# RWKV-7 attention into a mixture of experts: early loads, order of two small products, and the last store, all changed

## The chip, the cores and the metric

The program runs on one core of a Trainium2 chip. The time is that of the device for one execution, in microseconds (us). Ten executions of the kernel before took 1162.47 to 1171.4 us, with a median of 1168.91.

Five engines run their own instruction streams and wait for each other through semaphores: TensorE (PE; its weight loads are listed apart as PEld), VectorE (DVE), ScalarE (ACT), GpSimd (POOL) and SyncE (SP), which here only issues DMAs. Matrix products go to PSUM, everything else lies in SBUF.

## The reference

Two blocks follow each other. The first is a recurrence over 768 tokens for 4 batches and 8 heads of 40 numbers; the second is a mixture of 4 experts over the resulting 3072 rows of 320 numbers.

```python
for t in range(S):                                   # r,k,v,w,a,b: (4, 8, 768, 40)
    y[:, :, t] = einsum('bhd,bhde->bhe', rt, state)
    Sa = einsum('bhde,bhe->bhd', state, at)
    state_decay = state * wt[:, :, None, :] - einsum('bhd,bhe->bhde', Sa, bt)
    state = state_decay + einsum('bhd,bhe->bhde', vt, kt)

x = y.transpose(0, 2, 1, 3).reshape(3072, 320)       # w1: (4, 320, 1024), w2: (4, 1024, 320)
p = domain_probs / (domain_probs.sum(-1, keepdims=True) + 1e-9)
for e in range(4):
    h = maximum(x @ w1[e], 0)
    out += p[:, e:e + 1] * (h @ w2[e])
```

All of it is float32.

## The kernel before, in words

**Units.** The 768 tokens are cut into 12 chunks of 64. A unit is one chunk of two batches, so that 2 x 64 tokens fill the 128 partitions; there are 24 units, two to a chunk. The recurrence is solved inside a chunk with matrix products, and the state of each batch is carried from chunk to chunk.

**Stages of a unit.** They are generators, advanced step by step by `run(gen, n)`.
- `within` (L338 on) needs nothing of the state. It loads nothing itself; it turns the inputs W, A, B, K, V, R of its unit (tiles `natW` and so on), forms decayed keys, and the score matrices F, ET and EV (products `pw`, `pg`, `pRT`, `pVT`, `pAT`, `pNT`, `pKT`, `pc`, `pfe`, `pev`).
- `substitute` (L440 on) inverts 32 x 32 triangles, on GpSimd for all units but the first two.
- `merge` (L490 on) joins the inverses to 64 x 64. Its first step transposes them on VectorE (`Qc`, `QTc`). Its second step is the product `pY` (L510), copied by ScalarE to `Yq` in two copies (L516). Its third step is the product `pQ` (L522), which reads `Yq`, copied by ScalarE into `QT` in two copies (L527).
- `step` (L530 on) goes on with the state. Its first step is the product `prn` (the state against the gathered keys, and the state turned), from which VectorE makes `RH`. Its second step is `psat`, which reads `RH` and `QT`; then `pxr`, `pdy`, and the new state and output.

**Experts.** The output of a unit (first two units) or of a chunk (later) goes through the mixture. `up` (L646 on) makes the hidden layer from one piece of the first weights (L238 loads a piece, 512 KB and twice 64 KB). Down weights are loaded once, 1280 KB an expert (L255). For chunks, the product with the down weights is done in seven half-size products instead of eight: `down_1` makes three of them, `down_2` four, each over the sums of `add_weights` and `add_h` (L763); the products are at L769, and VectorE adds them, scaled by the gate, to the output tile `osb` (L680). The expert work is cut into pieces in the list `todo`; `mix(n)`, called by `gap`, puts n of them between the steps of the recurrence.

**What sets the order.** The program text, for the most part: instructions go to each engine in the order in which they are written, with some moved by a scheduler, and those in `keep_in_program_order` fixed. In the loop over u, iteration u advances `within` of unit u + 2 (`w`), `merge` (`m`) and the first two steps of `step` (`s_next`) of unit u + 1, and the rest of `step` of unit u. For u < 5 (`early`) the merge is placed later than for u of 5 and above.

**Loads.** All DMAs before are issued by SyncE, in one queue, in order. Eight semaphores are used in turn, so that a DMA is issued only when the eighth one before it has landed. Weights and attention inputs of the first units share that queue. `load_probs` (L206) loads the probabilities.

**The end.** After the loop, the last chunk's last expert runs `down_2`: products `p75` and `p26`, two additions each, then `store` (L682 on), two DMAs (one a batch) for each of the two output tiles.

Of the kernel before, what the change touches and what calls it, by code (L numbers as in the profile page):

```python
# [15 lines left out]
def kernel(  # L16
# [34 lines left out]
    nc = tc.nc  # L51

    B, H, S, D = r.shape
    E, DM, F = moe_w1.shape
    P = 128
    L = 64
# [11 lines left out]
    def big(name):  # L68
# [6 lines left out]
        out=ident[:], in_=ident[:], pattern=[[1, P]], compare_op=ALU.is_equal, fill=0.0,  # L75
# [5 lines left out]
    for t, n, op in ((upf, L, ALU.is_gt), (diagf, Q, ALU.is_equal)):  # L81
        nc.vector.memset(t[:], 1.0)
        for q in range(P // n):
            o = slice(q * n, (q + 1) * n)
            nc.gpsimd.affine_select(
                out=t[o], in_=t[o], pattern=[[1, n]], compare_op=op, fill=0.0, base=0, channel_multiplier=-1,
# [132 lines left out]
    def load_piece():  # L219

        k = len(pieces)
        e, x = k // 2 % E, k % 2
        if k in in_sums:
            t = sums[in_sums[k]]
        else:
            t = sb.tile([P, PIECE], FP32, name="w1p", tag="w1p", bufs=2)
        q = Piece()
        q.main = t[:, 0:2 * HF * P].rearrange("p (g c) -> p g c", g=2)
        q.last = t[:, 2 * HF * P:PIECE].rearrange("p (f c) -> p f c", c=P)
        cols = slice(x * HF * P, (x + 1) * HF * P)  # L230
        moves = [(q.main, moe_w1[e, 0:2 * P, cols].rearrange("(g p) c -> p g c", p=P))]
        for i in range(2):
            half_cols = slice((2 * x + i) * HF // 2 * P, (2 * x + i + 1) * HF // 2 * P)
            moves.append(
                (q.last[i * DT:(i + 1) * DT], moe_w1[e, 2 * P:DM, half_cols].rearrange("d (f c) -> d f c", c=P))
            )
        for to, src in moves:
            tc.keep_in_program_order(nc.sync.dma_start(out=to, in_=src))  # L238
        pieces.append(q)
# [14 lines left out]
    def load_w2(e):  # L254
        tc.keep_in_program_order(nc.sync.dma_start(out=w2_sb[e][:], in_=moe_w2[e].rearrange("(f p) d -> p f d", p=P)))  # L255
# [416 lines left out]
    def scale(q, e, minus=False):  # L672
        return (minus_gate if minus else gate)[:, q.c, q.bp, e:e + 1]

    def add(to, p, sc, start=False):

        if start:
            nc.vector.tensor_scalar(out=to, in0=p, scalar1=sc, scalar2=None, op0=ALU.mult)
        else:
            nc.vector.scalar_tensor_tensor(out=to, in0=p, scalar=sc, in1=to, op0=ALU.mult, op1=ALU.add)  # L680

    def store(q, osb):  # L682
        for i in range(2):
            row = q.b[i] * S + q.c * L
            nc.sync.dma_start(out=out[row:row + L, :], in_=osb[i * L:(i + 1) * L, :])

    def outputs():
        return sb.tile([P, DM], FP32, name="osb", tag="osb", bufs=2)
# [35 lines left out]
    def of_w2(e, q, x):  # L724
        return w2_sb[e][:, q * HF:(q + 1) * HF, x * HD:(x + 1) * HD]

    def of_sums(e, n):
        return sums[e][:, n * HF * HD:(n + 1) * HF * HD].rearrange("p (f d) -> p f d", d=HD)
# [14 lines left out]
    def mixture_of_chunk(qs, xT):  # L743

        hs, a_sums, osb = {}, {}, []
        at = 2 * E * (qs[0].c + 1)

        def ups(e, x):
            hs[e, x] = up(at + 2 * e + x, xT, 2 * P, P)
            used(at + 2 * e + x + 1)  # L750

        def of_h(e, s, x):
            return hs[e, x][:, :, s * P:(s + 1) * P]

        def add_h(e):
            a = {(s, x): of_h(e, s, x) for s in range(2) for x in range(2)}
            for n, x, y, op in (
                (1, a[0, 0], a[1, 1], ALU.add), (7, a[0, 1], a[1, 1], ALU.subtract),
                (5, a[0, 0], a[0, 1], ALU.add), (2, a[1, 0], a[1, 1], ALU.add),
                (6, a[1, 0], a[0, 0], ALU.subtract),  # L760
            ):
                t = a_sums[e, n] = sb.tile([P, HF, P], FP32, name=f"a{n}")
                nc.vector.tensor_tensor(out=t[:], in0=x, in1=y, op=op)  # L763

        def products(name, *terms):
            p = ps.tile([P, len(terms) * HD], FP32, name=name, tag="mm", bufs=3)
            for n, (a, b) in enumerate(terms):
                for f in range(HF):
                    nc.tensor.matmul(  # L769
                        out=p[:, n * HD:(n + 1) * HD], lhsT=a[:, f, :], rhs=b[:, f, :],  # L770
                        start=(f == 0), stop=(f == HF - 1),
                    )
            return p

        left, right, wide = slice(0, HD), slice(HD, DM), slice(0, DM)

        def down_1(e):
            p = products(
                "p431", (of_h(e, 1, 1), of_w2(e, 1, 0)), (of_h(e, 0, 0), of_w2(e, 0, 1)),
                (a_sums[e, 1], of_sums(e, 0)),  # L780
            )
            if e == 0:
                osb.extend(outputs() for _ in qs)

            for q, o in zip(qs, osb):
                add(o[:], p[:, wide], scale(q, e), e == 0)
            for q, o, cols in zip(qs, osb, (left, right)):
                add(o[:, cols], p[:, DM:DM + HD], scale(q, e))

        def down_2(e):  # L790
            p75 = products("p75", (a_sums[e, 7], of_sums(e, 2)), (a_sums[e, 5], of_w2(e, 1, 1)))
            p26 = products("p26", (a_sums[e, 2], of_w2(e, 0, 0)), (a_sums[e, 6], of_sums(e, 1)))
            for q, o, p, cols, n in ((qs[0], osb[0], p75, left, 1), (qs[1], osb[1], p26, right, 0)):
                add(o[:], p[:], scale(q, e))
                add(o[:, cols], p[:, n * HD:(n + 1) * HD], scale(q, e, minus=True))
            if e == E - 1:
                for q, o in zip(qs, osb):
                    store(q, o)


        before = last[:]
        for e in range(E):
            todo.append(lambda e=e: ups(e, 0))
            if before:
                todo.append(before[0])
                todo.append(lambda e=e: ups(e, 1))
                todo.append(lambda e=e, then=before[1]: (then(), add_h(e)))
            else:
                todo.append(lambda e=e: (ups(e, 1), add_h(e)))
            before = [lambda e=e: down_1(e), lambda e=e: down_2(e)]  # L810
        last[:] = before

    todo, last = [], []
# [1 line left out]
    def mix(n):  # L815

        for piece in todo[:n]:
            piece()
        del todo[:n]

    def run(gen, n=99):
        for _ in range(n):
            if next(gen, gen) is gen:
                break
# [21 lines left out]
    keep_warm(4)  # L846
    run(ws[0], 1)
    load(units[1], "ABKVR")
    for n in range(4):
        load_piece()  # L850
        if n == 1:
            load_w2(0)
    load_probs()
    run(ws[1], 1)
    run(ws[0], 2)
# [3 lines left out]
    m, s = merge(units[0]), begin_step(0)  # L859
    run(m, 1)  # L860
    run(ws[0])
    load(units[2], "WVR")
    load_w2(1)
    run(ws[1], 1)
    keep_warm(36)
    run(ws[1], 2)
# [13 lines left out]
    m, s = merge(units[1]), begin_step(1)  # L880
# [18 lines left out]
    for u in range(1, NU):  # L899
        q = units[u]  # L900
        m = s_next = w = iter(())
        if u + 1 < NU:
            m, s_next = merge(units[u + 1]), begin_step(u + 1)
        if u + 2 < NU:
            w = within(units[u + 2])

        def gap(n, pieces=None):
            at = 4 * u + n
            run(sum_ops, sums_at.get(at, 0))
            mix((1 if at in sparse else 2) if pieces is None else pieces)  # L910

        run(w, 1)
        run(w_next)
        run(s, 1)
        gap(0)


        early = u < 5
        if early:
            run(s, 1)  # L920
        run(w, 1)
        run(s)
        if u == 1:
            mixture_of_unit(q)
        elif q.bp:
            mixture_of_chunk(units[u - 1:u + 1], chunks_x[q.c])
        run(w, 1)
        if not early:
            run(m, 1)
        gap(1)  # L930

        if u + 3 < NU:
            load(begin(u + 3), srcs)
        run(w, 2)
        if not early:
            run(m, 1)
            run(s_next, 1)
            run(m)
        gap(2)

        if early:
            run(m, 1)
        run(w, 1)
        if not early:
            run(s_next, 1)
        if u + 2 < NU:
            substitute(units[u + 2], nc.gpsimd)
        if early:
            run(m, 1)
            run(s_next, 1)  # L950
            run(m)
            gap(3, 1)
            run(s_next, 1)
            mix(0 if 4 * u + 3 in sparse else 1)
        else:
            gap(3)
        s, w_next = s_next, w
# [31 lines left out]
```

## Time and profile before

| | |
|---|---|
| median of ten executions | 1168.91 us |
| profiled execution | 1170.02 us |
| its span, first to last instruction | 1168.3 us |
| mean granted clock of TensorE | 0.987 |
| TensorE busy | 1140.0 us (98%) |
| VectorE, ScalarE, GpSimd busy | 693.7, 385.5, 470.4 us |
| read from HBM | 97.04 MB |

The profile describes one execution. A wait is listed as "engine tile line <- what ended it: us in total, times, longest". A timeline line has start, length, engine, line, instruction, "out <- in", shapes and a count, and in brackets the idle time of the engine just before. Busy time of TensorE counts a product from its start to a modelled end; products overlap, so that the sum of lengths is more than the time. The clock is that which the chip granted to TensorE, where 1.00 is full speed.

### The profile page before, as it was taken

What the parts mean: (1) busy time and instruction counts of PE and PEld (TensorE: products, weight loads), DVE (VectorE), ACT (ScalarE), POOL (GpSimd) and SP (SyncE); (2) the same over time, 40 slices, a digit from 0 to 9 for tenths busy, and PEclk for the clock granted to TensorE, in tenths of its full rate; (3) what the DMA queues carried; (4) which work ended last, traced back from release to release, by engine and by line L of the source; (5) the groups of instructions that cost most, each with busy time, mean ns of one, the idle gap of its engine ahead of it and who ended that gap; (6) DMA issues with size and microseconds to landing.
All of it is one profiled execution on the core that took longest, in us unless ns stands there. A gap on an engine that the chain in (4) does not pass through costs nothing.

```text
span 1168.3 us, 38755 instructions
## 1 busy us (share of the span) xinstructions
PE 1140.0 (98%) x16400; PEld 1018.4 (87%) x16400; DVE 693.7 (59%) x1465; ACT 385.5 (33%) x961; POOL 470.4 (40%) x1218
## 2 busy tenths in 40 slices
PE   7898999999999999999999999999999999999998
PEld 6787887789898998989989998989989898998887
DVE  7565447766566656756655756666566567543333
ACT  2332444333333333342333333333323423321110
POOL 4005645562542733624625526427336255250000
PEclk8899999999999999999999999999999999999999
DMA  4695424323333243333333342332433331221330
GB/s 67 177 284 107 109 60 106 84 65 97 79 91 86 76 114 73 89 93 85 98 95 81 92 103 59 105 84 79 109 76 91 92 101 51 76 87 52 103 91 12
DMA packets 218693, 107.45 MB, mean 92 GB/s; under 512 B 163688, under 2 KB 191896, under 8 KB 218520
## 3 DMA queue, kind: packets, MB, share of 16 engines
q1 hardware_dynamic: 218520, 104.97, 34.8%
q8 instruction: 130, 2.13, 0.8%
q14 instruction: 43, 0.35, 0.1%
HBM read 97.04 MB, written 3.93 MB: 86 GB/s over the span
## 4 chain that ended last, share of the span: by engine, by line
PE 92%; DMA 2%; SPq 2%; ACT 2%; issue 1%; DVE 1%; DVEq 0%; ACTq 0%
PE ph L662 29%; PE p L769 29%; PE ph L654 9%; PE pdy L327 3%; PE po L703 2%; PE pfe L327 2%; PE psat L327 2%; SPq L188 2%; PE prn L327 2%; PE pxr L327 2%; PE pQ L522 1%; PE pc L327 1%; PE pY L510 1%; PE pev L327 1%; DMA w<-in_moe_w_dram 1%
## 5 line engine op out<-in xcount | busy, mean ns | idle before, releaser
L662 PE MATMUL ph<-xT,w1p 128*128 128x256 f32 (+1 forms) x1520 | 343.3, 379 | 0.0
L471 POOL TENSOR_TENSOR Z<-M,Z 128x62 f32<-128x62 f32 (+7 forms) x352 | 168.7, 479 | 405.7 <-DVE M L464 379.8
L662 PEld LDWEIGHTS ph<-xT,w1p 128*128 128x128 f32 x1520 | 274.4, 191 | 62.6 <-issue 25.2
L763 DVE TENSOR_TENSOR a<-hs 128x512 f32<-128x512 f32 x220 | 154.6, 720 | 190.9 <-ACT hs L667 190.9
L484 POOL TENSOR_TENSOR Z<-Z 128x31 f32<-128x31 f32 (+7 forms) x704 | 241.6, 343 | 55.2
L667 ACT ACTIVATE hs<-ph 128x512 f32<-128x512 f32 (+1 forms) x208 | 117.1, 564 | 304.2 <-PE ph L662 303.7
L769 PE MATMUL p<-sums,a 128*128 128x160 f32 x1056 | 164.8, 299 | 0.0
L680 DVE SCALAR_TENSOR_TENSOR osb<-p,gate,osb 128x320 f32<-128x320 f32 (+1 forms) x242 | 108.2, 485 | 92.5 <-PE p L769 88.3
L769 PEld LDWEIGHTS p<-sums,a 128*128 128x128 f32 x1056 | 152.9, 190 | 2.2
L654 PE MATMUL ph<-xT,w1p 64*128 64x256 f32 (+1 forms) x760 | 110.4, 397 | 0.6 <-ACT hs L667 0.6
L769 PE MATMUL p<-w,hs 128*128 128x160 f32 x704 | 102.9, 299 | 0.0
L769 PE MATMUL p<-w,a 128*128 128x160 f32 x704 | 102.8, 299 | 0.0
L769 PEld LDWEIGHTS p<-w,hs 128*128 128x128 f32 x704 | 100.2, 190 | 2.2
L769 PEld LDWEIGHTS p<-w,a 128*128 128x128 f32 x704 | 98.0, 190 | 0.0
L503 POOL COPY QT<-QTc 32x256 f32<-32x256 f32 x96 | 38.8, 404 | 107.1 <-DVE QTc L497 97.3
L654 PEld LDWEIGHTS ph<-xT,w1p 64*128 64x128 f32 x760 | 67.9, 187 | 13.1 <-issue 2.1
L448 DVE STREAM_TRANSPOSE M<-blocks 128x1024 f32<-128x1024 f32 x24 | 47.0, 1957 | 30.7 <-ACT blocks L445 30.0
L365 DVE RECIPROCAL gp<-gp 128x320 f32<-128x320 f32 x24 | 51.4, 2140 | 0.0
L419 ACT COPY F<-pfe 128x256 f32<-128x256 f32 x48 | 15.5, 375 | 90.7 <-PE pfe L327 90.7
L369 ACT COPY RT<-pRT 128x512 f32<-128x512 f32 x24 | 14.1, 586 | 93.4 <-PE pRT L295 93.3
L595 ACT COPY RS<-pxr 64x256 f32<-64x256 f32 x88 | 32.2, 366 | 34.6 <-issue 25.3
L327 PE MATMUL pdy<-VC,k_tok 64*64 64x104 f32 (+1 forms) x768 | 39.5, 263 | 2.5 <-issue 2.5
(143 smaller groups left out, 1428.2 us busy)
## 6 DMA issues: line engine op xcount, KB each, us to landing
w1p<-in_moe_w_dram SPq DMA_DIRECT2D x95, 512.0 KB
w1p<-in_moe_w_dram SPq DMA_DIRECT2D x190, 64.0 KB
w<-in_moe_w_dram SPq DMA_DIRECT2D x4, 1280.0 KB
sums<-in_moe_w_dram SPq DMA_DIRECT2D x9, 512.0 KB
natW<-in_w_dram SPq DMA_DIRECT2D x48, 80.0 KB
natA<-in_a_dram SPq DMA_DIRECT2D x48, 80.0 KB
natB<-in_b_dram SPq DMA_DIRECT2D x48, 80.0 KB
natK<-in_k_dram SPq DMA_DIRECT2D x48, 80.0 KB
```

Source lines behind the costliest of these rows:

```text
L327: nc.tensor.matmul(out=p[row][half(col), lo + at * out_cols:lo + (at + 1) * out_cols], lhsT=lhsT, rhs=rhs, start=(n == 0), stop=(n == len( ...
L365: nc.vector.reciprocal(out=gp[:], in_=gp[:])
L448: ins = nc.vector.transpose(out=M[:], in_=cols)
L471: ins = eng.tensor_tensor(out=Z[:, 1:3, 0:n, j + 1:Q], in0=M[:, j:j + 2, None, j + 1:Q].to_broadcast([P, 2, n, m]), in1=Z[:, here, 0:n, j: ...
L484: eng.tensor_tensor(out=z[:, 0], in0=z[:, 0], in1=z[:, x], op=ALU.add)
L503: ins = nc.gpsimd.tensor_copy(out=q.QT[quarter(i), :, quarter(i % 2)], in_=QTc[quarter(i)])
L654: nc.tensor.matmul(out=ph[i][:, f, :], lhsT=w1.last[i * DT:(i + 1) * DT, f, :], rhs=xT[i * DT:(i + 1) * DT, 2, :], start=(f == 0), stop=False,
L662: nc.tensor.matmul(out=ph[i][:, f, :], lhsT=w1.main[:, g, at * P:(at + 1) * P], rhs=xT[:, g, :], start=False, stop=(g == 1 and f == HF // ...
L667: nc.scalar.activation(out=h[:, i * HF // 2:(i + 1) * HF // 2, 0:n], in_=ph[i][:], func=ACTF.Relu,)
L680: nc.vector.scalar_tensor_tensor(out=to, in0=p, scalar=sc, in1=to, op0=ALU.mult, op1=ALU.add)
L763: nc.vector.tensor_tensor(out=t[:], in0=x, in1=y, op=op)
L769: nc.tensor.matmul(out=p[:, n * HD:(n + 1) * HD], lhsT=a[:, f, :], rhs=b[:, f, :], start=(f == 0), stop=(f == HF - 1),)
```

## The change

Three things are done, in one edit.
1. In the prologue, the first four pieces of the first weights and the down weights of the first expert are no longer loaded ahead of the probabilities. They are loaded, with the second expert's down weights, after W, V and R of the third unit (`units[2]`).
2. In the loop, for u of 5 and above, the first step of `step` (`prn`) is placed ahead of the second step of `merge` (`pY`), and the third step of `merge` (`pQ`) is placed behind `gap(2)`. For u < 5 the order stays as it is. In the built program no other product changes its place, but for four products of `up`, in the last iteration that has a merge, that come between `pQ` and `psat`. ScalarE's copies follow their products. ScalarE's copy of the third unit's V also comes earlier: behind the copies of the first unit's `pst`, ahead of those of the second unit's `pAT`, `pNT` and `pKT`.
3. For the last expert of the last chunk, `p26` is made as two products, `p2` and `p6`; the second output tile is stored in a left and a right half, the left one before `p6` is added. One of the two DMAs of the right half is issued by ScalarE.

```diff
-    def store(q, osb):
-        for i in range(2):
+    def store(q, osb, cols=slice(0, DM), second=nc.sync):
+        for i, eng in enumerate((nc.sync, second)):
             row = q.b[i] * S + q.c * L
-            nc.sync.dma_start(out=out[row:row + L, :], in_=osb[i * L:(i + 1) * L, :])
+            eng.dma_start(out=out[row:row + L, cols], in_=osb[i * L:(i + 1) * L, cols])
...
+        def down_2_at_end(e):
+            p75 = products("p75", (a_sums[e, 7], of_sums(e, 2)), (a_sums[e, 5], of_w2(e, 1, 1)))
+            p2 = products("p2", (a_sums[e, 2], of_w2(e, 0, 0)))
+            p6 = products("p6", (a_sums[e, 6], of_sums(e, 1)))
+            add(osb[0][:], p75[:], scale(qs[0], e))
+            add(osb[0][:, left], p75[:, right], scale(qs[0], e, minus=True))
+            store(qs[0], osb[0])
+            add(osb[1][:, left], p2[:], scale(qs[1], e))
+            add(osb[1][:, right], p2[:], scale(qs[1], e, minus=True))
+            store(qs[1], osb[1], left)
+            add(osb[1][:, right], p6[:], scale(qs[1], e))
+            store(qs[1], osb[1], right, nc.scalar)
...
     load(units[1], "ABKVR")
-    for n in range(4):
-        load_piece()
-        if n == 1:
-            load_w2(0)
     load_probs()
...
     load(units[2], "WVR")
-    load_w2(1)
+    for e in range(2):
+        load_piece()
+        load_piece()
+        load_w2(e)
     run(ws[1], 1)
...
         run(w, 2)
         if not early:
+            run(s_next, 1)
             run(m, 1)
-            run(s_next, 1)
-            run(m)
         gap(2)
 
-        if early:
-            run(m, 1)
+        run(m, 1)
         run(w, 1)
```

More of the change, by code (lines that the diff above doesn't have):

```diff
@@ L809, in mixture_of_chunk @@
                 todo.append(lambda e=e: (ups(e, 1), add_h(e)))
-            before = [lambda e=e: down_1(e), lambda e=e: down_2(e)]
+            second = down_2_at_end if (qs[0].end and e == E - 1) else down_2
+            before = [lambda e=e: down_1(e), lambda e=e, second=second: second(e)]
         last[:] = before
```

## The prediction

> **What bounds the kernel now.** I read the page first, then the waits of TensorE, then windows and timelines around those waits.
>
> ```profile
> PE 1140.0 (98%) x16400; PEld 1018.4 (87%) x16400; DVE 693.7 (59%) x1465; ACT 385.5 (33%) x961; POOL 470.4 (40%) x1218
> PEclk8899999999999999999999999999999999999999
> q8 instruction: 130, 2.13, 0.8%
> ```
>
> TensorE is busy for 1140.0 of 1168.3 us. The edits remove no matrix product, so they can only touch the 28.3 us of idle time, the time at half clock, and the tail. The third line matters later: 130 packets, 2.13 MB, so 16 KB each, on the instruction queue for some 33,200 TensorE instructions, about 256 instructions a packet.
>
> ```profile
> PE pQ L522 <- issue: 3.9, 3, 1.4
> PE pdy L327 <- issue: 2.5, 1, 2.5
> PE pRT L295 <- DMA natR<-in_r_dram: 2.2, 2, 1.4
> PE pw L295 <- DMA natW<-in_w_dram: 0.9, 1, 0.9
> ```
>
> "issue" means that the profile shows nothing waited for. Each of these four waits has an instruction packet beside it: at 41.23 us (2.55), 229.79 (1.43), 315.66 (1.28) and 863.39 (1.15) TensorE restarts 1.4 to 1.6 us after the end of such a packet. They are waits for instructions. The other two lines are inputs of the fourth unit, at 91.4 and at 101.6 to 104.2 us. Around the early waits the windows show the granted clock:
>
> ```profile
> 39.40:42.80 3.40, 1.64 (x46) 1.23 (x42) 0.90 (x4) 0.18 (x1) 0.00 (x0) 1.00 1.02 315
> 42.80:46.20 3.40, 2.42 (x24) 2.17 (x25) 1.34 (x5) 0.00 (x0) 0.00 (x0) 0.50 0.47 124
> 46.20:49.60 3.40, 3.40 (x18) 3.40 (x17) 0.46 (x3) 1.75 (x3) 0.00 (x0) 0.50 0.35 55
> 100.80:104.20 3.40, 1.17 (x12) 0.63 (x7) 3.26 (x9) 0.46 (x1) 2.78 (x8) 1.00 0.18 32
> 104.20:107.60 3.40, 3.40 (x16) 3.40 (x17) 2.75 (x4) 1.17 (x2) 2.87 (x7) 0.50 0.81 253
> ```
>
> After the stretch, the columns are busy time of PE, PEld, DVE, ACT and POOL, granted clock, DMA share and GB/s. A stretch that is idle for 1.76 of 3.40 us is followed by two at clock 0.50, one idle for 2.23 by one.
>
> **Part 1, the loads.** SyncE's issues in order of time:
>
> ```profile
> 29.48 1.79 SPq L238 DMA_DIRECT2D w1p<-in_moe_w_dram  x3
> 38.26 5.86 SPq L206 DMA_DIRECT2D sums<-in_moe_domain_probs_dram  x4
> 50.10 4.41 SPq L188 DMA_DIRECT2D natR<-in_r_dram  x6
> 54.97 0.40 SPq L255 DMA_DIRECT2D w<-in_moe_w_dram  x1
> 84.48 2.87 SPq L188 DMA_DIRECT2D natW<-in_w_dram  x2
> 97.77 4.92 SPq L188 DMA_DIRECT2D natR<-in_r_dram  x6
> ```
>
> Moved: four pieces (12 issues) and the first down weight (1) go behind probs (4) and W, V, R of unit 2 (14). Probs issued 0.3 to 0.6 us apiece apart from their waits, say 2.0; the 14 took 44.22 to 54.52 us, 10.1 to 10.3. The first piece is then issued at 29.5 + 2.0 + 10.1 = 41.6 us. Before, it landed 5.1 us after issue and the first down weight 12.4 after that issue: now 46.7 and 54.0. TensorE wants them, as follows. The fetch that stopped it at 41.23 us ran while the queues moved 315 GB/s; the same unit-2 loads, where they stand before, move 56 GB/s over 44 to 55 us. So the stall (2.55) goes, and with it the half clock of 42.8 to 49.6 us (5.82 us busy, 2.9 lost): `ph` is ready at 52.82 - 5.4 = 47.4 us and `po` at 54.0. Both weights come just in time. ACT now copies unit 2's V ahead of the AT, NT and KT copies; V lands by about 39.5 us, before the product of unit 0 that frees its buffer ends (41.75), and the copy takes 0.46: hidden under the transposes.
>
> What is late next is the DMA stream. The weights for units 0 and 1 now run without a break from 41.6 us until natW of unit 3, whose second issue, at 86.73 us, waits for the last down weight. Before, the same stream had holes: against the 327 GB/s of 70 to 88 us, 55 to 58 us and 62 to 70 us fall short by 4.0 to 5.2 us of transfer. It loses 2.7 again, because the light stretch in front of it grows from 9.4 us (45.6 to 55.0) to 12.1 (29.5 to 41.6). So natW and natR of unit 3 land 1.3 to 2.5 us earlier, say 2.2, and TensorE, 5.4 early, waits some 3.7 us at `pw` (0.86 before). It then runs at half clock while natR is still being issued, and hardly waits again at `pRT`; the half clock of 104.2 to 107.6 us (3.40 busy, 1.7 lost) then does not come. I take 2.2 + 1.3 of the 1.7 = **-3.5 us**. Ends: -6 (stream at full rate, both clocks saved) and -0.5 (a stream with no hole less, and the half clock stays).
>
> The Trainium skill (TensorE: Matmul & The Clock Gate, Part 1) gives the half rate after an idle window of about 3.4 us. The trace disagrees: 1.76 us idle was enough. By the rule no half clock would come here at all, and part 1 would be worth the 2.2 alone.
>
> **Part 2, the order of `pY` and `pQ`.** Units 6 to 23 (18 times): `pY` now follows `prn`, and `pQ` goes behind two pieces of expert work. The stretch before:
>
> ```profile
> 313.42 0.69 PE L510 MATMUL pY<-QTc,F 32*32 32x32 f32 x32
> 314.04 0.68 PE L327 MATMUL prn<-state,AT 64*64 64x40 f32 x32
> 314.53 0.67 PE L327 MATMUL prn<-ident,state 64*64 64x64 f32 x32
> 315.13 0.53 PE L522 MATMUL pQ<-Yq,Qc 32*32 32x32 f32 x21
> 316.94 0.37 PE L522 MATMUL pQ<-Yq,Qc 32*32 32x32 f32 x11 [1.28 <-issue]
> ```
>
> In these units `pQ` waits for `Yq` nowhere: `prn` lasts 1.09 us and covers two ACT copies (0.75) and two hand-overs (about 0.2). The move saves nothing there. Its new risk is `psat`, which needs the QT copies; only `pfe` stands between, 0.98 us, with the same two copies of 0.75. Equal covers, no wait, so 0 per unit; if the hand-over were longer, 0.1 to 0.3 each. Unit 23 has no `pfe`; four `ph` (0.5 us) are put there: +0.4 once. PSUM buffers turn in fives, and each is freed earlier than wanted in either order.
>
> What does change is where dense small products meet a fetch. Laid along the instruction count, packets start at the earliest 103 instructions before a multiple of 256 and stalls begin 193 to 203 past it: a fetch has 296 instructions to land. Fetches take 2.4 to 4.1 us from request to restart in most of the trace (7 to 9 in the loaded prologue). Before, the densest run (`pc` to `pQ`) passes 296 instructions in 2.65 and 2.67 us where it fits a block worst, and exactly these two stalled, 2.43 us together. Reordered, with the durations of before, four blocks fall into `pQ`, `pfe`, `psat` with 2.28, 2.41, 2.78 and 2.92 us to spare. At 3.1 to 3.2 us, the latency seen at those four blocks, they stall 2.4 us together; at 3.6, 4.0. Against 2.43 lost now: 0 to +1.6, say +0.6. Part 2: **+1.0** (-2.4 to +6; the upper end has stalls drop the clock).
>
> The skill (Runtime: NRT & Kernel Launch, Instruction fetch mechanics) has the 16 KiB block of 256 instructions, as here, and calls its crossing mostly hidden. Four crossings here cost 6.4 us. By the page, this term is 0.
>
> **Part 3, the tail.**
>
> ```profile
> 1162.67 3.28 SPq L685 DMA_DIRECT2D out_dram<-osb  x4
> 1163.84 0.55 DVE L680 SCALAR_TENSOR_TENSOR osb<-p,gate,osb 128x320 f32<-128x320 f32 x1 [1.20 <-PE p L769]
> 1164.43 0.38 DVE L680 SCALAR_TENSOR_TENSOR osb<-p,minus_gate,osb 128x160 f32<-128x160 f32 x1
> ```
>
> The last two stores start at 1164.84 and 1165.35 us, behind both additions, and the span ends 2.95 after the last start. Now the left half is added while `p6` runs, and one addition of 128x160 (0.38) follows, to 1164.22. SyncE ends the first two stores at 1163.80, issues the left half (0.5 + 0.6) and starts the last at 1164.99: 0.36 earlier. ACT issues its store at about 1164.25; no DMA issue by ACT is in the trace, and it would have to take 1 us more than SyncE's 0.6 to end last. **-0.4** (-0.7 to +0.5).
>
> **Sum.** -3.5 + 1.0 - 0.4 = -2.9 us. The profiled execution took 1170.02 us (span 1168.3, 1.7 around it) and stands 1.1 over the median of ten, 1168.91; its stalls are of a kind that most executions should share, so I subtract from the median: **1166.0 us**. A measurement here tells about 0.2%, 2.3 us, from no change.
>
> **The rivals.**
> (a) The transfers bind anyway: natR of unit 3 lands when it did, and part 1 is worth at most the 0.5. Then -0.5 + 1.0 - 0.4: 1169.0. For it: the gain is a difference of two estimates of 3 to 5 us. Against it: the holes at 55 to 58 and 62 to 66 us.
> (b) Faster still: the fetch stall at 229.79 us, whose neighbour wait of 0.82 for `QTc` and half clock to 237.3 us cost 1.43 + about 3 more, goes too when the loads around it shift. -2.9 - 4.4: 1161.6. For it: the lowest run shown is 1162.47. Against it: the work there keeps its order.
> (c) Slower by fetches: the four blocks of part 2 stall 1.3 us each (+2.8 net) and two of them bring two windows of half clock (3.4 each): +9.6 instead of +0.6, so 1175.0. It decides from +5.8 on. For it: clock 0.50 after 1.76 us idle. Against it: 1.28 and 1.15 brought none.
> (d) Slower by QT: `psat` waits in all 18 units. With no cover, at 36.2 us, it waited 0.6; 0.35 each, +6.3, gives 1172.3; it decides from 0.3. Against it: `pQ` with the same cover never waited.
>
> **How the numbers follow.** Forecast 0.48 (its own range 1163 to 1168; 0.37 of it faster by over 0.2%, 0.11 within), (a) 0.22 (0.19 within, 0.03 slower), (b) 0.14, (c) 0.10, (d) 0.06. Faster 0.51, same 0.30, slower 0.19. The range reaches to (b) and past (a): 1161.5 to 1171.5.
>
> **What would show it.** Part 1: no gap at 41 us, clock 1.00 to past 80 us, a wait of 3 to 4 us at `pw`, natR's last issue near 100 us instead of 102.08. Part 2: `issue` waits at `psat` or `ph` in place of `pQ`, none for QT. Part 3: last store at 1.2 us after TensorE's end. The forecast is wrong if the stream is slower than 327 GB/s, or if the fetch at 41 us stalls although the queues are light.

## The result and the profile after

| | before | after |
|---|---|---|
| median | 1168.93 us (40 executions) | 1164.04 us (12 executions) |
| span of the profiled execution | 1168.3 us | 1163.5 us |
| mean granted clock | 0.987 | 0.988 |

The ratio is 0.9962, with a 95% interval of 0.9953 to 0.9972: 3.3 to 5.5 us less. A repetition on another occasion gave 1163.85 us against 1168.32, ratio 0.9964 (0.9949 to 0.9979). The change made the kernel faster by 0.38%: 4.9 us less than before by the medians, where the forecast, 1166.0 us, was 2.9 us less.

The busy time and the clock, from the page of the changed kernel:

```profile
PE 1136.6 (98%) x16400; PEld 1015.8 (87%) x16400; DVE 693.9 (60%) x1466; ACT 385.7 (33%) x961; POOL 472.4 (41%) x1218
PEclk7999999999999999999999999999999999999999
```

TensorE does the same 16400 products in 3.4 us less busy time. So not all of the gain is idle time removed: some is clock, and some is products that take less. The prediction had allowed only for idle time, half clock and the tail.

Its waits (what waited, for what: us in total, times, longest):

```profile
PE pw L295 <- DMA natW<-in_w_dram: 4.3, 1, 4.3
PE pQ L522 <- issue: 1.4, 1, 1.4
PE ph L654 <- issue: 1.4, 2, 1.2
PE pRT L295 <- DMA natR<-in_r_dram: 0.7, 1, 0.7
PE psat L327 <- issue: 0.7, 1, 0.7
PE psat L327 <- ACT QT L527: 0.6, 1, 0.6
```

The wait of 2.5 us at `pdy` is gone, and `pw` of the fourth unit waits 4.3 us where it waited 0.9. Two of three waits for instructions ("issue", called fetch stalls below) at `pQ` went; there are three new ones at `ph` and `psat`. For `QT`, `psat` waits once, 0.6 us, and that is the wait at 36 us that the kernel before had too.

SyncE's issues of the load stage in order of time:

```profile
29.47 1.78 SPq L206 DMA_DIRECT2D sums<-in_moe_domain_probs_dram  x4
41.32 2.61 SPq L238 DMA_DIRECT2D w1p<-in_moe_w_dram  x3
81.81 3.90 SPq L188 DMA_DIRECT2D natW<-in_w_dram  x2
95.99 3.87 SPq L188 DMA_DIRECT2D natR<-in_r_dram  x6
```

The weights begin at 41.3 us. W of the fourth unit is asked for at 81.8 us, and its second half lands at 90.6; R is asked for from 96.0 us, and its last part lands at 102.4.

The windows around the waits (stretch; its length; busy time of PE, PEld, DVE, ACT, POOL; granted clock; DMA share; GB/s):

```profile
86.46:90.72 4.26, 0.00 (x0) 0.03 (x1) 1.46 (x3) 0.00 (x0) 2.45 (x9) 1.00 1.00 136
91.40:94.80 3.40, 3.40 (x74) 3.06 (x75) 2.20 (x6) 1.59 (x6) 2.96 (x6) 0.51 0.49 82
228.00:231.40 3.40, 3.40 (x19) 2.32 (x14) 2.84 (x6) 1.36 (x4) 1.98 (x4) 0.50 0.20 32
231.40:234.80 3.40, 3.40 (x10) 2.68 (x9) 0.00 (x0) 0.60 (x1) 2.69 (x10) 0.50 0.14 21
```

In the first row TensorE is idle for 4.26 us while the DMA engines are busy throughout. One window of half clock follows, and two more follow the fetch stall at 226 us. The windows of half clock at 42.8 to 49.6 and at 104.2 to 107.6 us do not occur any more.

The starts of the same products in both profiles place the gain. Against before, the first `ph` is 4.9 us earlier (47.88), `pw` of the fourth unit 1.5, and everything from 105 to 226 us 3.3 to 3.7. Behind the half clock at 228 us it is 3.3, then it grows evenly, with steps at the fetch stalls, to 5.6 us at 1025 us. Unit 23 takes 0.5 back, and the tail 0.3.

### The profile page after: what moved, and what is told of

Same layout as the page of the kernel before. It is cut to its first block, busy times and chain, and to the rows that moved or that the text cites. A ratio compares the mean times of both kernels' runs of the same rounds, so it can differ in the third digit from the quotient of the medians.

```text
span 1163.5 us, 38763 instructions
## 1 busy us (share of the span) xinstructions
PE 1136.6 (98%) x16400; PEld 1015.8 (87%) x16400; DVE 693.9 (60%) x1466; ACT 385.7 (33%) x961; POOL 472.4 (41%) x1218
## 4 chain that ended last, share of the span: by engine, by line
PE 91%; DMA 2%; SPq 2%; DVE 2%; ACT 2%; issue 1%; DVEq 0%; ACTq 0%
PE ph L662 29%; PE p L769 29%; PE ph L654 9%; PE pdy L327 3%; PE psat L327 2%; PE pfe L327 2%; PE po L703 2%; PE pxr L327 2%; SPq L188 2%; PE prn L327 2%; PE pQ L522 1%; PE pc L327 1%; PE pY L510 1%; DMA w<-in_moe_w_dram 1%; PE pev L327 1%; PE pRT L295 1%
## 5 line engine op out<-in xcount | busy, mean ns | idle before, releaser
L527 ACT COPY QT<-pQ 32x256 f32<-32x256 f32 x48 | 17.4, 363 | 83.7 <-PE pQ L522 83.2
```

## The experiments

Theory A says: the gain is the shorter load stage, plus a cheaper order of the small products, and the load stage is now bound by the order of one DMA stream. Rival B says that the load stage makes all of it; rivals C to G belong to single runs (they are not the rivals (a) to (d) of the prediction).

**Part 1 alone.** The kernel before, with the loads of the change and nothing else:

```diff
-    for n in range(4):
-        load_piece()
-        if n == 1:
-            load_w2(0)
     load_probs()
...
     load(units[2], "WVR")
-    load_w2(1)
+    for e in range(2):
+        load_piece()
+        load_piece()
+        load_w2(e)
```

> Part 1 alone on the kernel before. Theory A (the gain of the change is the sum of a shorter load stage and a cheaper order of the small products): 3.4 us less, about 1165.5 us, with the wait of about 4.3 us at `pw` of unit 3 as in the changed kernel, no gap at 41 us, and the steady stage unchanged: `issue` waits at `pQ` near 312 and 860 us, as before. Rival B (the load stage makes the whole gain, and the order nothing): 4.9 us less, about 1164.0 us.

Measured: 1165.89 us against 1169.54, ratio 0.9969 (0.9957 to 0.9982), so 3.6 us less (2.1 to 5.0). Its load-stage waits:

```profile
PE pw L295 <- DMA natW<-in_w_dram: 5.1, 2, 4.8
PE pRT L295 <- DMA natR<-in_r_dram: 1.2, 1, 1.2
PE po L703 <- DMA w<-in_moe_w_dram: 1.1, 1, 1.1
```

The waits for W and R are those of the changed kernel, and `po` also waits 1.1 us for the first down weight, which the prediction had "just in time". No gap at 41 us. The two stalls at `pQ` near 314 and 862 us stay (0.61 and 1.15). The median is where theory A put it; rival B's 4.9 lies at the edge of the interval.

**Part 2 alone.** The kernel before, with the new order in the loop:

```diff
         if not early:
+            run(s_next, 1)
             run(m, 1)
-            run(s_next, 1)
-            run(m)
         gap(2)
-        if early:
-            run(m, 1)
+        run(m, 1)
```

> Part 2 alone on the kernel before. Theory A: every unit from 6 to 23 is 0.10 us shorter, because the products of 64x64 blocks now stand together and TensorE changes the block shape once less per unit (the last product of `pc` takes 0.11 us more ahead of a 32x32 product than ahead of a 64x64 one); 18 times 0.10, minus 0.4 for fetch stalls that move, plus 0.5 for unit 23: 1.5 to 1.8 us less, about 1167.3 us. Rival B: no difference (within 0.5 us). The recorded forecast of this term: 1.0 us more.

Measured: 1168.52 us, ratio 1.0004 (0.9991 to 1.0016): between 1.1 us less and 1.9 more. Theory A's 1.5 to 1.8 us less lies outside that interval; rival B's no difference and the recorded forecast of 1.0 us more lie inside, and the times do not tell these two apart. The profile shows a shorter unit and something against it. From one `pdy` to that of the second unit after it, two units take 90.88 us in the kernel before (394.13 to 485.01) and 90.66 us here (389.65 to 480.31), so the shorter unit is there. Against it stand fetch stalls at `ph` (596 us, 0.83) and at `psat`:

```profile
825.38 0.32 PE L327 MATMUL psat<-RH,QT 64*64 64x40 f32 x5 [1.43 <-issue]
```

and behind that one a window runs at half clock:

```profile
823.40:826.80 3.40, 1.97 (x51) 1.54 (x42) 1.22 (x4) 1.51 (x7) 0.00 (x0) 1.00 0.32 88
826.80:830.20 3.40, 3.40 (x9) 2.69 (x9) 1.92 (x1) 1.33 (x4) 0.00 (x0) 0.51 0.35 122
```

The stall and the window cost 1.4 + 1.7 us. Stalls at these places differ from one execution to the next (0.66 us at `psat` in the first profile of the changed kernel, 1.03 in its repetition, neither with a window of half clock). That they hide the gain in the median is not shown: this execution itself took 1167.18 us, less than the median.

**Which half of the reordering makes a unit shorter.** The changed kernel with `pY` put ahead of `prn` again, `pQ` left in its new place:

```diff
         if not early:
-            run(s_next, 1)
             run(m, 1)
+            run(s_next, 1)
         gap(2)
```

> The changed kernel with `pY` ahead of `prn` again in units 6 to 23, while `pQ` stays where the change put it. It tells which half of the reordering makes a unit shorter. Theory A (each change of the block shape costs about 0.1 us): `pc`, `pY`, `prn` go 64, 32, 64 again, one change more, so units from 6 on take 45.48 us again in place of 45.38, 0.10 each. Rival E (the gain comes from `pQ`, no longer waiting for `Yq`): the units stay at 45.38 us.

Measured: one execution, 1164.82 us. From one `pdy` to that of the second unit after it, two units take 91.00 us here (432.42 to 523.42), 90.68 in the changed kernel (435.16 to 525.84) and 90.87 in the kernel before (439.53 to 530.40). The gain is gone, and 0.06 us a unit more than it, so it comes from where `pY` stands, and rival E falls. First the timeline of the changed kernel, then of this one, at the same place of a unit (start, length, engine, line, product, block, shape, count):

```profile
446.18 0.69 PE L327 MATMUL pc<-RT,VT 64*64 64x64 f32 x32
446.70 0.63 PE L327 MATMUL prn<-state,AT 64*64 64x40 f32 x32
447.14 0.67 PE L327 MATMUL prn<-ident,state 64*64 64x64 f32 x32
447.74 0.69 PE L510 MATMUL pY<-QTc,F 32*32 32x32 f32 x32
```

```profile
443.44 0.69 PE L327 MATMUL pc<-RT,VT 64*64 64x64 f32 x32
444.06 0.69 PE L510 MATMUL pY<-QTc,F 32*32 32x32 f32 x32
444.69 0.68 PE L327 MATMUL prn<-state,AT 64*64 64x40 f32 x32
445.17 0.67 PE L327 MATMUL prn<-ident,state 64*64 64x64 f32 x32
```

Starts tell it, not lengths. `pc` hands over after 0.52 us to a product of the same block, 64x64, and after 0.62 us to one of 32x32. It is not `prn` or `pY` alone: in the load stage of the changed kernel `pc` hands over after 0.52 us to `pfe` (64x64, at 45.15 us) and after 0.62 us to `ph` (64x128, at 110.20 us). The first half of `prn` takes 0.44 us behind `pc` and 0.48 behind `pY`. In `psat` 0.08 us is lost again. In the new order a unit changes the block four times between `pc` and `psat` (64 to 32, to 128, to 32, to 64), in the other two orders five times.

**Part 3 alone.** The kernel before, with the last expert in parts (`down_2_at_end` and the new `store`).

> Part 3 alone on the kernel before. Theory A: TensorE's end to the end of the span is 4.8 us in place of 4.5, so 0 to 0.3 us more; the five stores on SyncE's queue stand back to back and the last one is issued 1.4 us after TensorE's end. The recorded forecast of this term: 0.4 us less. Either is under what the times can tell, so the profile decides: the time from the end of the last product to the end of the span.

Measured: 1168.75 us, ratio 1.0000 (0.9984 to 1.0017): nothing that the times can tell. From TensorE's end to the span's end the kernel before takes 4.5 us, this run 5.3. The changed kernel takes 4.8 in its first profile and 4.3 in the repetition. Of the nine profiles on record with this end, the other six have 4.3 too. The stores of this run:

```profile
1159.91 4.04 SPq L685 DMA_DIRECT2D out_dram<-osb  x5
1161.50 0.55 ACTq L685 DMA_DIRECT2D out_dram<-osb  x1
```

SyncE issues five stores in 4.04 us here, in 3.61 in the first profile of the changed kernel and in 3.06 in the repetition. The last store starts 1.37 us behind TensorE's end in all three (1.55 before), and its issue takes 0.55 us in the repetition, 1.1 in the first profile and 1.5 here. So the part is worth 0.2 us in seven of nine profiles, and loses 0.3 and 0.75 in the two where that last issue is slow.

**A better end.** The changed kernel, with every second store on ScalarE:

```diff
-            store(qs[0], osb[0])
+            store(qs[0], osb[0], wide, nc.scalar)
...
-            store(qs[1], osb[1], left)
+            store(qs[1], osb[1], left, nc.scalar)
```

> The changed kernel with every second one of its six last stores on ScalarE's queue in place of the last alone. Theory A (the end is set by SyncE's row of issues at 0.55 us each, of which the last started 0.9 us after the last addition): the two last stores are issued side by side right behind the last addition, and TensorE's end to the span's end is 3.8 to 4.1 us in place of 4.8. Rival F (the landing of the stores sets it, whoever issues them): 4.6 to 4.8 us.

Measured: one execution, 1164.28 us; TensorE's end to the span's end is 3.5 us, better than expected.

```profile
1157.64 2.05 SPq L685 DMA_DIRECT2D out_dram<-osb  x3
1157.64 2.08 ACTq L685 DMA_DIRECT2D out_dram<-osb  x3
1158.82 0.38 DVE L680 SCALAR_TENSOR_TENSOR osb<-p,gate,osb 128x160 f32<-128x160 f32 x1 [0.41 <-PE p L769]
```

The last two issues start together, 0.45 us behind TensorE's end. Rival F falls: SyncE's row of issues set the end.

**The order of the load stream.** The changed kernel, with the loads of the fourth unit (`units[3]`) moved forward in three steps. The third is shown; the first moves W and puts R and V ahead of A, B, K, the second moves W, R, V.

```diff
     load(units[2], "ABK")
     load_piece()
+    load(begin(3), "W")
...
     run(m)
+    load(units[3], "RVABK")
     mix(1)
...
-    load(begin(3), srcs)
```

> The changed kernel, with the loads of unit 3 asked for in another order: its W behind the fifth weight piece, ahead of three down weights and pieces that TensorE uses later, and R and V ahead of A, B and K. Theory A (the load stage is bound by the order of one stream, not by its bytes): the wait of 4.3 us at `pw` and the one of 0.7 at `pRT` go, and with them the half clock behind the first; 4 to 6 us less than the changed kernel, about 1159 us. Rival C (the bytes bind): the wait goes to a weight piece or to A, B, K, and at most 1 us is won over the changed kernel, 1163 to 1164 us.

Measured: 1161.00 us, ratio 0.9933 (0.9913 to 0.9953), so about 3 us under the changed kernel, where theory A had 4 to 6. The profile has no wait of note at `pw` (0.2), and two for V (0.88 and 1.06 us), with a window of half clock behind them:

```profile
PE pVT L295 <- DMA natV<-in_v_dram: 1.9, 2, 1.1
PE pw L295 <- DMA natW<-in_w_dram: 0.2, 1, 0.2
```

> As early3, with R and V of unit 3 also ahead of the two weight pieces (the tenth and eleventh) that TensorE uses only from about 110 us. Theory A: the waits of 0.88 and 1.06 us at `pVT` near 96 us and the half clock behind them go: 2.5 to 3.5 us less than early3, about 1158 us. Rival C (the bytes bind): the tenth piece, A, B or K then come late, with a wait of 2 us or more at a `ph` near 105 us or at `pAT`, and the time stays at about 1161 us.

Measured: 1160.93 us, ratio 0.9936 (0.9914 to 0.9958). The profiled execution took 1158.32 and shows the waits for V gone and 1.18 us at `pNT` (for `n_tok`, which needs B). The times show no gain over the step before, as rival C had it, but not the wait of 2 us or more that it named; with six executions each, 2 us can hide in that. The third step decides.

> As early3b, with A, B and K of unit 3 as well ahead of the tenth and eleventh weight piece. Theory A: the wait of 1.2 us at `pNT` (for B) near 102 us goes, no other comes, since the tenth piece is wanted only near 107 us: 5 to 6 us less than the changed kernel, 1158 to 1159 us. Rival C: the tenth piece is late and `ph` near 107 us waits 1 us or more: no gain over early3b, 1160 to 1161 us.

Measured: 1157.65 us, ratio 0.9908 (0.9886 to 0.9930): 6 us under the changed kernel in the same comparison. In its profile, no DMA wait of the fourth unit is left and the clock is 1.00 from 42.3 to 219.8 us:

```profile
86.57 0.60 PE L295 MATMUL pw<-ident,natW 128*128 128x128 f32 x4
95.68 0.60 PE L295 MATMUL pRT<-ident,natR 128*128 128x128 f32 x4
```

The same bytes in another order remove the wait. So the load stage of the changed kernel was bound by what the one queue was asked for first: four transfers (the last down weight and three pieces), which the changed kernel uses only from 104 us on, were ahead of the W that it wanted at 86. Rival C falls.

**The fetch stalls.** The changed kernel, with small products put into the wait at `pw` that move all later instructions against the blocks of 256 in which they are fetched; 23 products are 92 instructions, 54 are 216:

```diff
         run(w, 1)
         run(w_next)
...
+        if u == 1:
+            shift = big("shift")
+            for _ in range(23):
+                ins = nc.tensor.matmul(
+                    out=shift[0:Q, 0:Q], lhsT=ident[0:Q, 0:Q], rhs=ident[0:Q, 0:Q], start=True, stop=True,
+                )
+                tc.keep_in_program_order(ins)
```

(It stands ahead of the two `run` lines.)

> The changed kernel, with 23 products of 32x32 (92 instructions, 0.5 us) put into the wait of 4.3 us at `pw` of unit 3, so that every later block of 256 TensorE instructions begins 92 instructions earlier in the work. Nothing else differs. Theory A (a fetch stalls where a block's last 296 instructions are dense): the stalls at `pQ` near 226 us (1.45, with 6.8 us of half clock), at `ph` near 370 and 596 and at `psat` near 824 go; new ones of 0.2 to 1.0 us stand near 120 (`pQ`), 456 (`psat`) and 780 us (`ph`). 2 to 5 us less than the changed kernel, 1159 to 1162 us. Rival D (the waits come from the memory or the queues, not from the place in the instruction stream): they stay where they are and the time is 1164.0 to 1164.5 us.

> As shift92 with 54 products (216 instructions, 1.2 us, inside the same wait). Theory A: stalls near 188 (`prn`), 227 (`pQ`, with its half clock), 284 (`ph`), 505 and 735 (`psat`), 960 us (`psat`), of 0.5 to 1.4 us each, 4 to 5 us together against 3.5 in the changed kernel: 1 to 3 us more than the changed kernel, 1165 to 1167 us. Rival D: the waits stay where they are, 1164.0 to 1164.5 us.

Measured with 92: 1161.35 us, ratio 0.9934 (0.9910 to 0.9959), though the profiled execution took 1163.99. With 216: 1165.42 us, ratio 0.9969 (0.9953 to 0.9985). The stalls of the first, then of the second:

```profile
120.91 0.98 PE L522 MATMUL pQ<-Yq,Qc 32*32 32x32 f32 x31 [0.77 <-issue]
158.52 0.60 PE L522 MATMUL pQ<-Yq,Qc 32*32 32x32 f32 x16 [0.53 <-issue]
551.86 0.70 PE L654 MATMUL ph<-xT,w1p 64*128 64x256 f32 x3 [0.42 <-issue]
```

```profile
189.34 0.33 PE L327 MATMUL prn<-ident,state 64*64 64x64 f32 x4 [1.04 <-issue]
227.74 0.53 PE L522 MATMUL pQ<-Yq,Qc 32*32 32x32 f32 x11 [0.60 <-issue]
279.14 1.02 PE L654 MATMUL ph<-xT,w1p 64*128 64x256 f32 x6 [0.61 <-issue]
506.96 0.31 PE L327 MATMUL psat<-RH,QT 64*64 64x40 f32 x3 [1.25 <-issue]
734.97 0.33 PE L327 MATMUL psat<-RH,QT 64*64 64x40 f32 x9 [1.20 <-issue]
```

With 92, the stalls at 226, 370, 596 and 824 us are all gone, and new ones stand at 120 and 778 us (0.97) as forecast; the one forecast at 456 did not come, those at 158 and 551 were not named. With 216, five of the six named places stalled (the one named at 284 us at 279), and the one at 960 did not. Nothing but the place in the instruction stream was changed for that work, so rival D falls. The profiles on record agree: counted along TensorE's instructions, its stalls of 0.3 us and more put down to "issue" all begin 193 to 195 past a multiple of 256, and end 1.2 to 1.7 us behind the end of an instruction packet.

**All together.** The third load order, the stores on two queues, and the 23 products.

> early3c, the stores of tail2 and the 23 small products of shift92 together. Theory A: the three causes lie at different places and add up: early3c's time, minus 0.8 for the stores, minus 1.5 to 4 for the fetch stalls (less the 0.5 that the products now cost, as no wait hides them): 1154 to 1157 us. Rival G (each only uncovers another wait): no better than early3c.

Measured: 1155.42 us against 1168.32, ratio 0.9897 (0.9877 to 0.9918): 12 to 13 us under the kernel before and 8 under the changed one. The stores add up as expected (3.5 us at the end). The fetch part does so only in part: the stall near 220 us is gone, but one of 1.58 us with two windows of half clock stands at 115 us instead, and the profiled span, 1155.4 us, is only 0.5 under that of the load order alone.

The changed kernel's repetition:

> The changed kernel once more, beside the other kernels of this comparison on the same chip: 1164 us, ratio to the kernel before 0.995 to 0.997. Its second profile tells which of its waits are in every execution (the one at `pw` of unit 3, by theory A, 4 to 5 us) and which come and go (the fetch stalls near 226, 370, 596 and 824 us: the same places, other lengths).

Measured: 1163.85 us. `pw` waits 4.82 us, `pRT` 0.61; the fetch stalls begin at 226.7 (1.48), 276.8 (0.12), 369.1 (0.21), 595.6 (0.55) and 822.9 us (1.03).

## Why the prediction was right, and where it was not

**Part 1, forecast -3.5: right, in size and in mechanism.** Part 1 alone measured -3.6. In the changed kernel the first piece was issued at 41.32 us (forecast 41.6) and landed at 46.56 (46.7). The first down weight landed at 52.92 (54.0), the wait at `pw` was 4.26 us (3.7, though the prediction's own terms, 0.86 + 5.4 - 2.2, give 4.1), and R's last issue was at 99.26 (near 100). `po` came 3.4 us earlier at 104.5, of which 1.8 is the earlier end of the wait for R and 1.6 the window at 104.2 to 107.6 us that is no longer at half clock: forecast 2.2 and 1.3. The two terms erred by 0.4 and 0.3 us in opposite ways, so that the sum came out this near is partly luck. Rival (a), that the transfers bind anyway, was half true: they do bind, but earlier. That this bound was one of order and not of bytes was not in the prediction; the third load order shows it. Nor did it see a second wait that the old order of loads can bring. In the profiles of parts 2 and 3 alone, `pev` near 52 us waits 2.41 and 2.63 us, because the copies of ScalarE that it needs stand behind one that waits for V of the third unit. Of part 2 alone:

```profile
53.12 0.46 ACT L398 COPY VC<-natV 128x320 f32<-128x320 f32 x1 [3.79 <-DMA natV<-in_v_dram]
54.37 0.31 PE L327 MATMUL pev<-VC,ET 64*64 64x40 f32 x2 [2.41 <-DVE ET L334]
```

With the new order of loads no profile has this wait: in the changed kernel that copy of V is made at 42.40 us.

**Part 2, forecast +1.0: the wrong sign in the profile.** The step that failed is "Equal covers, no wait, so 0 per unit". The waits were judged rightly (none for `QT`, so rival (d) falls), but a unit's own time was taken as fixed under reordering, and it was not: a unit became 0.10 us shorter, 18 times, 1.8 to 1.9 us in all. The rows in the prediction's own fence held the clue: from `pY` over `prn` to `pQ` the block goes from 32x32 to 64x64 and back. The Trainium skill (TensorEngine Tiling (Array Packing), Tiling Modes, Key Properties) says that changing the tiling mode drains TensorE. It gives no price; here, `pc` takes 0.10 to 0.11 us more ahead of another block.

The other two terms of part 2 held. Fetch stalls behind 240 us: 2.43, 1.75 and 1.60 us in the profiles with the old order, 2.08, 1.91 and 1.98 in those with the changed kernel's loads and order, 2.0 to 2.9 in the other runs with the new order and no instructions put in. The means are 1.93, 1.99 and, over all seven with the new order, 2.2: 0.1 to 0.3 us more, inside the 0 to +1.6 given, under the +0.6 taken. By the Trainium skill (Runtime: NRT & Kernel Launch, Instruction fetch mechanics), which calls the crossing of a block mostly hidden, the term was 0, about as near. But it is a difference of two sums of about 2 us, and the runs with 92 and 216 instructions show crossings that cost 0.4 to 1.3 us each, among dense products. Unit 23: +0.5 for +0.4. Together part 2 is about -1.1 us in the profiles (-1.85 + 0.3 + 0.5). What it is in the times stays open: alone it measured +0.5 us with an interval from -1.1 to +1.9, which holds the forecast too, and the changed kernel stands only 0.6 to 0.8 us under part 1 alone, with overlapping intervals. The three parts alone sum to 3.1 us less, the whole measured 4.9; the intervals are wide enough for that.

**Part 3, forecast -0.4: too good.** The last store was to start 0.36 us earlier and starts 0.18 us earlier, because SyncE issues its fourth and fifth store only after the third, 0.55 to 0.6 us each. ScalarE's store, the one with no row before, took 0.54 us and was never last. In seven of nine profiles that makes the tail 0.2 us shorter; where SyncE's last issue takes 1.1 or 1.5 us, the part costs 0.3 or 0.75.

**The rivals.** (b) did not come: the stall near 229 us is in both profiles of the changed kernel (1.45 and 1.48). It is not in those of parts 2 and 3 alone, which have the old loads, so it comes and goes. (c) did not come in the changed kernel: three of the four blocks stalled, 0.21, 1.21 and 0.66 us, and none dropped the clock; but part 2 alone shows one that did. The error of the whole, 2 us, is the size of that of part 2 (2.1).

## What to carry to other kernels

When a long wait on a DMA stands in a stage where the queue is full, compare each transfer ahead of it with the time at which its bytes are first used, before counting bytes: here the order of the same transfers was worth 6 us. When small products of different block shapes are reordered, count the changes of shape and price them by the start-to-start time of the last product ahead of each; a reordering that removes no wait can still shorten the work. A stall put down to "issue" beside an instruction packet belongs to a place in the instruction stream; a few dozen instructions more ahead of it move it, and the stall may land on a worse place.

## What was not expected of the hardware

- A change of the block shape (64x64 to 32x32 or 64x128) costs about 0.1 us of TensorE time, paid in the product ahead of it: `pc` takes 0.62 us to hand over, against 0.52 ahead of another 64x64 block.
- Whether a stall halves the clock is not told by its length. Stalls of 1.02 us (part 3 alone, at 312 us), 0.77 (92 instructions, at 120, with 0.27 of another wait just ahead) and 1.43 (part 2 alone, at 824) were followed by a window of half clock; one of 1.60 (the first load order, at 592) and one of 1.28 us (the same run, at 821) were not. What decides it was not settled.
- The first fetch stall in the load stage varies with the old load order: 2.55 us at 41 us in the first profile, 1.94 at 40 in the one of part 2 alone and 1.61 at 42 in the one of part 3 alone. With the new order of loads, the longest fetch stall between 38 and 50 us in any profile is 0.31 us (at 44.8, with `pY` first).
